# Where the fifth form of a Strassen-like product is summed in the first block of a gated Fourier/SwiGLU kernel, and where raw blocks of x lie

## The chip, the cores and the metric

One core of a Trainium2 chip runs the whole program. The metric is the device time of one execution in microseconds; before the change its median over three runs is 712.95 (712.55 to 713.23). One more execution was recorded by the hardware profiler: it took 713.02, and the instructions in its trace span 711.3.

TensorE (PE in the profile) multiplies, VectorE (DVE) and ScalarE (ACT) prepare operands and read results, GpSimd (POOL) and SyncE (SP) issue the DMAs here.

## The reference

```python
g = sigmoid((x * gate_w).sum(-1, keepdims=True))
a = x @ Wd_re.T ; b = x @ Wd_im.T               # transform along the hidden dimension
y = Ws_re @ a - Ws_im @ b                       # along the sequence, real part
h = silu(x @ w1) * (x @ w3) ; m = h @ w2        # SwiGLU
out = g * y + (1 - g) * m
```

x has 2048 rows of 512 columns, w1 and w3 are 512 x 1376, w2 is 1376 x 512, Ws 2048 x 2048 and Wd 512 x 512, all in float32.

## The kernel before

**Products.** Every float32 operand is split into a high part (ScalarE copies it into the matmul's reduced float32 format, L108) and a low part (VectorE subtracts, L111). A product is then three matmuls: high by high, high by low, low by high, in this order (`mm3`, L117). Each matmul has 512 moving columns. The large products are done in a Strassen-like way: of a 2 x 2 partition of the operands, seven products of sums of blocks instead of eight of blocks.

**Stages.** First the SwiGLU's w1 and w3 products with the gate run (`gate_up`, up to about 217 us of the trace). Then follow eight blocks: four F blocks (the transform along the sequence, applied to x), two H blocks (the w2 product) and two Y blocks (the transform along the hidden dimension). The change is in F block 0, which begins at 217.9 us.

**A block.** A block is the list `CHAIN` (L587): P1 with form B11, P5 with T1, P6 with T2, P3 with B22, P7 with T3, P2 with B21, P4 with T4. The moving operand comes from the DFT matrix `cc`: the raw blocks B11, B12, B22, B21, each in four pairs q = 0 to 3 (tiles 128 x 1024, 512 KB, called `B` in the profile). A step is one product with one q: 12 matmuls. So block 0 has steps 0 to 27: P1 is steps 0 to 3, P5 4 to 7, P6 8 to 11, P3 12 to 15, P7 16 to 19, P2 20 to 23, P4 24 to 27. The parts of a form's step, tile `zo`, have four buffers.

**Order.** The order of each engine is written out by hand. After step m's matmuls, `advance(m)` (L673) loads raw blocks for up to eight steps ahead if buffers are free, does the sum for step m + 4 (`sum_c`) and the split for step m + 3 (`split_c`). Other work is tied to a step of a block with `at` and comes ahead of the step's matmuls.

**Forms.** T1 = B12 + B11 and T2 = T1 + B22 are formed in B12's buffer by VectorE. T3 = B12 + B22. In blocks 1 to 7 VectorE forms it as T2 - B11 in B11's buffer (L649). In block 0 B11's buffer is given back as early as T1, and T3 is formed by a DMA: once B22 is split, GpSimd's queue issues a load of B12 from `cc` that adds into B22's buffer (L663). ScalarE splits that buffer for steps 16 to 19 when the DMA has landed.

**Raw blocks of x.** The stationary operands of block 0's last products and of later blocks are made from the eight raw blocks of x, `xs0` to `xs7` (128 x 1024, source `xn`): `load_a2(p)` at step 4 + p issues the load on SP's queue into a buffer of the common list `F4` (`wide`), and `make_a2(p)` at step 8 + p does the sum S3 on VectorE (128 x 256, L168), then ScalarE and VectorE split 512 and 256 columns into `a2_p` (called `a` in the profile). The three parts are in `forms2` (L165).

**Results.** At the end of P3 (step 15), P7 (step 19) and later products VectorE adds partial results and multiplies by the gate (`zu`, L862 and L772; tags u2, u3, c21, s1, p5 of the pool `ut`).

Of the kernel before, what the change touches and what calls it, by code (L numbers as in the profile page):

```python
# [7 lines left out]
F32 = mybir.dt.float32  # L8
# [4 lines left out]
P = 128  # L13
# [8 lines left out]
NG = NST // 2  # L22
# [10 lines left out]
def fnet_swiglu_gate_kernel(  # L33
# [20 lines left out]
    nc = tc.nc  # L54

    def pool(name, bufs, side, space=None):
        kw = {} if space is None else {"space": space}
        cm = tc.tile_pool(name=name, bufs=bufs, side=side, reuse_waits="tile", **kw)
        return cm, cm.__enter__()
# [30 lines left out]
    def take(places, shape, dtype, name):  # L90
        p, tag = at = places.pop(0)
        t = p.tile(shape, dtype, tag=tag, name=name)
        HELD[id(t)] = t, places, at
        return t

    def wide(name):
        return take(F4, [P, 1024], F32, name)

    def parts(name):
        return take(ZO, [P, 2, 4, 256], F32R, name)  # L100

    def free(*tiles):
        for t in tiles:
            _, places, at = HELD.pop(id(t))
            places.append(at)
# [7 lines left out]
    def split(hi, lo, src):  # L113
        high(hi, src)
        low(hi, lo, src)
# [18 lines left out]
    def flat(ap):  # L134
        return ap.rearrange("p a n -> p (a n)")
# [22 lines left out]
    def sums1_here(r):  # L158
# [3 lines left out]
        for d, v, w in ((a21, a22, a11), (a12, a12, a21)):  # L162
            nc.vector.scalar_tensor_tensor(d, v, -1.0, w, op0=ALU.mult, op1=ALU.subtract)

    def forms2(r, t2):  # L165

        r = r.rearrange("p (a n) -> p a n", a=4)
        nc.vector.tensor_sub(r[:, 0], r[:, 1], r[:, 0])  # L168
        split(flat(t2[:, 0, 0:2]), flat(t2[:, 1, 0:2]), flat(r[:, 2:4]))
        split(t2[:, 0, 2], t2[:, 1, 2], r[:, 0])  # L170

# [363 lines left out]
    A1, A2, XR = [], [], {}  # L535
# [17 lines left out]
    for n in range(NI):  # L553
        if n in W2_AT:
            p = W2_AT.index(n)
# [4 lines left out]
        if n in A1_AT:  # L560
            p = A1_AT.index(n)
# [13 lines left out]
    do(at_end, NI - 2, load_a, NG - 1)  # L575
    do(early, NI - 1, lambda: sums1_here(XR[NG - 1]))
    do(mid, NI - 1, lambda: split_c(0))
    do(at_end, NI - 1, lambda: split_c(1))


# [12 lines left out]
    NQ = [{"F": NG // 2, "H": NP2 // 2, "Y": KD // 2}[k] for k in KIND]  # L593
# [5 lines left out]
    NEED.append((("B11", 0, 0), ("B21", 1, 0), ("B12", 2, 1), ("B22", 3, 1)))  # L599
    PLACE = {"T1": "B12", "T2": "B12", "T4": "B12", "T3": "B11"}  # L600

    DONE = {"T4": "B21"}, {"T4": "B12", "B22": "B22", "T3": "B11"}
    DONE0 = {"T1": "B11", "T4": "B21"}, {"T4": "B12", "T3": "B22"}
    LEAD = 3
# [4 lines left out]
    RAW, ZT = {}, {}  # L609
# [6 lines left out]
    def block(blk, k, q):  # L616
        if KIND[blk] == "F":
            return cc[blk, ("B11", "B12", "B22", "B21").index(k), q]
        if KIND[blk] == "H":
            return hsp[blk - NTB, ("B11", "B12", "B21", "B22").index(k), q]  # L620
        return z_rows(2 * (blk - NTB - 2) + (k in ("B12", "B22")), 2 * (k in ("B21", "B22")) + q)

    def cols(blk, q, form):

        return 512 if KIND[blk] == "H" and q == NQ[blk] - 1 and form in ("B21", "B22", "T4") else 1024

    def done(m, j):
        blk, q, k, form = STEPS[m]
        b = (DONE if blk else DONE0)[j].get(form)
        if b:  # L630
            free(RAW.pop((blk, b, q)))

    def place(blk, form):
        return "B22" if form == "T3" and not blk else PLACE.get(form, form)

    def sum_c(m):


        if not 0 <= m < len(STEPS):
            return  # L640
        blk, q, k, form = STEPS[m]
        b = {"T1": "B11", "T2": "B22", "T4": "B21"}.get(form)
        if b:
            n = cols(blk, q, b)
            t = RAW[blk, PLACE[form], q][:, :n]
            nc.vector.tensor_add(t, t, RAW[blk, b, q][:, :n])  # L646
        elif form == "T3" and blk:
            t = RAW[blk, "B11", q]
            nc.vector.tensor_sub(t, RAW[blk, "B12", q], t)  # L649
        done(m, 0)  # L650

    def split_c(m):

        if not 0 <= m < len(STEPS):
            return
        blk, q, k, form = STEPS[m]
        src = RAW[blk, place(blk, form), q]
        ZT[m] = parts(f"zo{m}")
        t = ZT[m].rearrange("p h a n -> p h (a n)")
        n = cols(blk, q, form)  # L660
        split(t[:, 0, :n], t[:, 1, :n], src[:, :n])
        if form == "B22" and not blk:
            nc.gpsimd.dma_start(src, block(blk, "B12", q), accum_op=ALU.add)  # L663
        done(m, 1)

# [7 lines left out]
    def advance(m):  # L673
        load_c(m + LEAD + AHEAD)
        sum_c(m + LEAD + 1)
        split_c(m + LEAD)
# [12 lines left out]
    ut_cm, ut = pool("ut", 1, "right")  # L689
    F4[:0] = [(f4_b, f"f4_{k}") for k in range(5 + LOOK, 13)]  # L690
    ZO[:0] = [(zo_b, f"zo_{k}") for k in range(2, 4)]
    def load_a2(p):

        XR[p] = wide(f"xs{p}")
        nc.sync.dma_start(XR[p], xn[p])

    def make_a2(p):
        A2.append(a2.tile([P, 2, 3, 256], F32R, tag=f"a2_{p}", name=f"a2_{p}"))
        forms2(XR[p], A2[p])
        free(XR.pop(p))  # L700

    GATES = {}

# [181 lines left out]
    def at(blk, n, f, *a):  # L885
        todo.setdefault(START[blk] + n, []).append((f, a))

    at(1, 1, load_score, 1)
    for p in range(NG):
        at(0, 4 + p, load_a2, p)  # L890
        at(0, 8 + p, make_a2, p)
    at(0, 4, gates, 0)
    at(1, 3, gates, 1)
    late = [(w2, w2sp, p) for p in range(len(W2_AT), NP2)] + [(dd, dsp, p) for p in range(KD)]
    for i, (src, sp, p) in enumerate(late):
        blk, b = 1 + i // 2, i % 2
# [85 lines left out]
```

## Time and profile before

| | us |
|---|---|
| median of three runs | 712.95 |
| the profiled execution | 713.02 |
| its span in the trace | 711.3 |
| TensorE busy in the span | 705.0 |
| VectorE busy | 600.9 |
| ScalarE busy | 369.4 |
| GpSimd busy | 67.5 |

The granted TensorE clock is full all through. Times in the views are microseconds from the span's start. A row of the timeline gives start, length, engine, source line, operation, tiles and a count; in brackets stands how long the engine was idle before, and what ended that. An operation's stated length can overlap the next one's start, so what it costs in a row of operations is the distance of the starts.

### The profile page before, as it was taken

How to read it: one execution, taken by the hardware profiler on the slowest of the kernel's cores; microseconds unless marked ns; L12 is line 12 of the kernel's file. 1: busy time of each engine (PE TensorE's matmuls, PEld its weight loads, DVE VectorE, ACT ScalarE, POOL GpSimd, SP SyncE). 2: the span in 40 equal slices, each digit the busy share in tenths (PEclk: the TensorE clock that was granted, in tenths of full speed). 3: DMA queues.
4: the chain of work that ended last, by engine and by line, in shares of the span. 5: the costliest groups of instructions: out<-in, count | busy, mean ns of one | idle time of the engine just before them, and what ended most of it. 6: DMA issues, size and time to landing. Idle time of an engine off the chain costs nothing.

```text
span 711.3 us, 8601 instructions
## 1 busy us (share of the span) xinstructions
PE 705.0 (99%) x3089; PEld 578.4 (81%) x3089; DVE 600.9 (84%) x729; ACT 369.4 (52%) x477; POOL 67.5 (9%) x122
## 2 busy tenths in 40 slices
PE   9999999999999999999999999999999999999997
PEld 5888888888888877888888888888888888888886
DVE  6979988787679889887999599969997896898985
ACT  6665555655445665354554553544445345445451
POOL 0011111221110010000110001100110000000000
PEclk9999999999999999999999999999999999999999
DMA  7585556599997498812496228915999971773932
GB/s 280 194 296 212 213 190 253 183 314 360 417 412 270 179 242 328 302 60 88 152 360 273 89 83 336 364 37 201 362 417 416 369 266 62 295 277 140 323 119 89
DMA packets 45980, 174.64 MB, mean 246 GB/s; under 512 B 5361, under 2 KB 5489, under 8 KB 42097
## 3 DMA queue, kind: packets, MB, share of 16 engines
q1 hardware_dynamic: 32464, 118.50, 45.5%
q0 software_dynamic: 13184, 55.07, 20.4%
q8 instruction: 24, 0.39, 0.2%
q10 hardware_dynamic: 288, 0.52, 0.2%
q14 instruction: 20, 0.16, 0.1%
HBM read 116.92 MB, written 57.16 MB: 245 GB/s over the span
## 4 chain that ended last, share of the span: by engine, by line
PE 91%; issue 5%; DMA 3%; DVE 0%; POOL 0%; ACT 0%; SPq 0%; POOLq 0%; ACTq 0%
PE P L119 61%; PE X L119 16%; PE Z L119 8%; PE Y L119 4%; PE C L119 2%; DMA B<-cc 1%; DMA p5g<-gs 1%; DMA xs_B<-xt 1%; DVE zo L111 0%; ACT zo L108 0%; POOL B L663 0%; DVE xo L111 0%; DVE zc L783 0%; ACT xo L108 0%; POOL gsp L723 0%
## 5 line engine op out<-in xcount | busy, mean ns | idle before, releaser
L119 PE MATMUL P<-zo,a 128*128 128x512 f32 x1344 | 306.6, 390 | 0.8 <-DVE zo L111 0.8
L119 PEld LDWEIGHTS P<-zo,a 128*128 128x128 f32 x1344 | 251.7, 188 | 55.5 <-DVE zo L111 3.3
L108 ACT ACTIVATE zo<-B 128x1024 fp32r<-128x1024 f32 (+1 forms) x182 | 188.9, 1044 | 180.9 <-PE P L119 93.3
L111 DVE TENSOR_TENSOR zo<-B,zo 128x1024 fp32r<-128x1024 f32 (+1 forms) x182 | 218.0, 1206 | 52.4 <-ACT zo L108 51.8
L119 PE MATMUL P<-zo,H 128*128 128x512 f32 x468 | 106.2, 389 | 0.0
L119 PEld LDWEIGHTS P<-zo,H 128*128 128x128 f32 x468 | 87.8, 188 | 18.2
L646 DVE TENSOR_TENSOR B<-B,B 128x1024 f32<-128x1024 f32 (+1 forms) x78 | 93.2, 1195 | 0.1
L119 PE MATMUL X<-xo,wb 128*128 128x512 f32 x378 | 92.6, 389 | 0.0
L119 PEld LDWEIGHTS X<-xo,wb 128*128 128x128 f32 x378 | 71.0, 188 | 14.7
L119 PE MATMUL P<-zo,Y 128*128 128x512 f32 x336 | 76.3, 389 | 0.0
L119 PEld LDWEIGHTS P<-zo,Y 128*128 128x128 f32 x336 | 63.1, 188 | 13.1
L319 POOL DMA_DIRECT2D hsp<-h x42 | 23.0, 548 | 126.7 <-DVE h L370 75.8
L119 PE MATMUL X<-xo,wa 128*128 128x512 f32 x126 | 32.3, 389 | 0.0
L119 PE MATMUL Z<-xo,wa 128*128 128x512 f32 x126 | 32.3, 390 | 0.0
L119 PE MATMUL Y<-xo,wa 128*128 128x512 f32 x126 | 32.2, 389 | 0.0
L119 PE MATMUL Z<-xo,wb 128*128 128x512 f32 x126 | 32.1, 389 | 0.0
L364 DVE TENSOR_TENSOR u<-u,X 128x512 f32<-128x512 f32 x21 | 14.4, 688 | 17.9 <-PE X L119 15.6
L858 ACT ACTIVATE zu<-P 128x512 f32<-128x512 f32 x32 | 19.0, 597 | 19.2 <-PE P L119 19.2
L119 PEld LDWEIGHTS Z<-xo,wa 128*128 128x128 f32 x126 | 23.6, 188 | 5.3 <-DVE xo L111 0.4
L119 PEld LDWEIGHTS Y<-xo,wa 128*128 128x128 f32 x126 | 23.7, 188 | 4.9
L119 PEld LDWEIGHTS X<-xo,wa 128*128 128x128 f32 x126 | 23.7, 188 | 4.9
L119 PEld LDWEIGHTS Z<-xo,wb 128*128 128x128 f32 x126 | 23.7, 188 | 4.9
(134 smaller groups left out, 558.3 us busy)
## 6 DMA issues: line engine op xcount, KB each, us to landing
B<-cc SPq DMA_DIRECT2D x64, 512.0 KB, 6.8
hsp<-h POOLq DMA_DIRECT2D x42, 256.0 KB, 3.6
B<-hsp SPq DMA_DIRECT2D x20, 512.0 KB, 10.4
wbsp<-wb POOLq DMA_DIRECT2D x8, 1024.0 KB, 4.4
wb<-wbsp SPq DMA_DIRECT2D x8, 1024.0 KB, 7.7
B<-zsp SPq DMA_DIRECT2D x16, 512.0 KB, 8.3
H<-w2sp SPq DMA_DIRECT2D x6, 1024.0 KB, 10.1
ws<-w SPq DMA_DIRECT2D x11, 512.0 KB, 6.9
```

Of the source, the lines that this page charges most:

```text
L108: nc.scalar.activation(hi, src, AF.Copy)
L111: nc.vector.tensor_sub(lo, src, hi.bitcast(F32))
L119: nc.tensor.matmul(ps, u, v, start=first and n == 0, stop=last and n == 2, skip_group_check=chain)
L319: nc.gpsimd.dma_start(hsp[g, b + k, j // 2, :, j % 2 * 512 : (j % 2 + 1) * 512], h)
L364: nc.vector.tensor_add(u4, u4, x)
L646: nc.vector.tensor_add(t, t, RAW[blk, b, q][:, :n])
L858: nc.scalar.activation(U[name][:, r], ps[r], AF.Copy)
```

## The change

1. `by_dma(blk, q)` is true only for block 0 with q = 0 and 1. For q = 2 and 3 T3 is now T2 - B11 by VectorE, as in other blocks; two of the four accumulating DMAs go. For these pairs B11's buffer is held until T3's split, and B22's is given back after its own split.
2. S3 of xs(p) moves from the head of `forms2` at step 8 + p to a function of its own, `sum2`, at step 7 + p.
3. xs0 and xs4 are loaded into the tile with tag u3 of the results' pool, xs1 and xs5 into c21; xs2, xs3, xs6 and xs7 stay in `F4`. The load of xs4 must wait until xs0 has been split, that of xs5 for xs1.

```diff
+    def sum2(r):
+        nc.vector.tensor_sub(r[:, :256], r[:, 256:512], r[:, :256])
     def forms2(r, t2):
         r = r.rearrange("p (a n) -> p a n", a=4)
-        nc.vector.tensor_sub(r[:, 0], r[:, 1], r[:, 0])
         split(flat(t2[:, 0, 0:2]), flat(t2[:, 1, 0:2]), flat(r[:, 2:4]))
         split(t2[:, 0, 2], t2[:, 1, 2], r[:, 0])
...
+    def by_dma(blk, q):
+        return not blk and q < NQ[0] // 2
     def done(m, j):
         blk, q, k, form = STEPS[m]
-        b = (DONE if blk else DONE0)[j].get(form)
+        b = (DONE0 if by_dma(blk, q) else DONE)[j].get(form)
         if b:
             free(RAW.pop((blk, b, q)))
-    def place(blk, form):
-        return "B22" if form == "T3" and not blk else PLACE.get(form, form)
+    def place(blk, q, form):
+        return "B22" if form == "T3" and by_dma(blk, q) else PLACE.get(form, form)
...
-        elif form == "T3" and blk:
+        elif form == "T3" and not by_dma(blk, q):
             t = RAW[blk, "B11", q]
             nc.vector.tensor_sub(t, RAW[blk, "B12", q], t)
...
-        src = RAW[blk, place(blk, form), q]
+        src = RAW[blk, place(blk, q, form), q]
...
-        if form == "B22" and not blk:
+        if form == "B22" and by_dma(blk, q):
             nc.gpsimd.dma_start(src, block(blk, "B12", q), accum_op=ALU.add)
...
     def load_a2(p):
-        XR[p] = wide(f"xs{p}")
+        XR[p] = (flat(ut.tile([P, 2, 512], F32, tag=("u3", "c21")[p % 4], name=f"xs{p}"))
+                 if p % 4 < 2 else wide(f"xs{p}"))
         nc.sync.dma_start(XR[p], xn[p])
     def make_a2(p):
         A2.append(a2.tile([P, 2, 3, 256], F32R, tag=f"a2_{p}", name=f"a2_{p}"))
-        forms2(XR[p], A2[p])
-        free(XR.pop(p))
+        r = XR.pop(p)
+        forms2(r, A2[p])
+        if p % 4 > 1:
+            free(r)
...
     for p in range(NG):
         at(0, 4 + p, load_a2, p)
+        at(0, 7 + p, lambda p=p: sum2(XR[p]))
+    for p in range(NG):
         at(0, 8 + p, make_a2, p)
```

## The prediction

> **What bounds the kernel now.** I read the page's first lines, then the waits of the engines in block 0, then the timeline of TensorE.
>
> ```profile
> span 711.3 us, 8601 instructions
> PE 705.0 (99%) x3089; PEld 578.4 (81%) x3089; DVE 600.9 (84%) x729; ACT 369.4 (52%) x477; POOL 67.5 (9%) x122
> ```
>
> TensorE sets the end: it is idle for 711.3 - 705.0 = 6.3 us, and a gain can come only from stalls inside its row of matmuls. An undisturbed row, out of the chain that ended last, gives the pace; three rows of TensorE's timeline (one window up to 271, one from there) show where it is broken.
>
> ```profile
> 203.09 2.72 PE X L119 x12
> ...
> 261.69 9.34 PE L119 MATMUL P<-zo,a 128*128 128x512 f32 x37
> ...
> 270.57 0.47 PE L119 MATMUL P<-zo,a 128*128 128x512 f32 x1
> 271.80 8.45 PE L119 MATMUL P<-zo,a 128*128 128x512 f32 x36 [0.76 <-DVE zo L111]
> ```
>
> Twelve matmuls, one step, take 2.72 us: 0.2267 us each. From 261.69 the 37 matmuls of the first row include the one at 270.57: 36 distances in 8.88 us, where 36 x 0.2267 = 8.16 would do, so 0.72 us was lost in small pieces; the next start, at 271.80, comes 1.23 after, 1.00 too late. Together **1.72 us** between steps 16 and 19. The matmul that starts at 271.80 is the second of step 19, the first that reads the step's low part. Without the stalls it would start at 270.08, and the second matmul of step m at 270.08 - 2.72 x (19 - m): step 16 at 261.92, step 17 at 264.64, step 18 at 267.36.
>
> Who is late? The waits between 241 and 272 us (waiting tile and line, releaser; total, times, longest), and one turn of VectorE's and ScalarE's timeline in the steps in which a raw block of x is prepared:
>
> ```profile
> ACT a L108 <- DVE xs L168: 7.8, 7, 1.1
> DVE zo L111 <- ACT zo L108: 4.2, 9, 0.5
> ACT zo L108 <- DMA B<-cc: 2.8, 1, 2.8
> ```
>
> ```profile
> 241.54 1.22 DVE L646 TENSOR_TENSOR B<-B,B 128x1024 f32<-128x1024 f32 x1
> 242.68 1.22 DVE L111 TENSOR_TENSOR zo<-B,zo 128x1024 fp32r<-128x1024 f32 x1
> 243.81 0.42 DVE L168 TENSOR_TENSOR xs<-xs 128x256 f32<-128x256 f32 x1
> 244.15 1.02 DVE L111 TENSOR_TENSOR a<-xs,a 128x512 fp32r<-128x512 f32 x2
> 245.67 1.23 DVE L111 TENSOR_TENSOR zo<-B,zo 128x1024 fp32r<-128x1024 f32 x1 [0.50 <-ACT zo L108]
> 246.81 0.42 DVE L168 TENSOR_TENSOR xs<-xs 128x256 f32<-128x256 f32 x1
> ...
> 248.67 1.23 DVE L111 TENSOR_TENSOR zo<-B,zo 128x1024 fp32r<-128x1024 f32 x1 [0.50 <-ACT zo L108]
> ...
> 266.66 1.22 DVE L111 TENSOR_TENSOR zo<-B,zo 128x1024 fp32r<-128x1024 f32 x1 [0.51 <-ACT zo L108]
> 267.80 1.28 DVE L862 TENSOR_TENSOR zu<-zu,P 128x512 f32<-128x512 f32 x2
> 269.00 1.29 DVE L772 TENSOR_TENSOR zu<-zu,gate 128x512 f32<-128x512 f32 x2
> 270.51 4.63 DVE L111 TENSOR_TENSOR zo<-B,zo 128x1024 fp32r<-128x1024 f32 x4 [0.23 <-ACT zo L108]
> ```
>
> ```profile
> 245.54 0.62 ACT L108 ACTIVATE a<-xs 128x512 fp32r<-128x512 f32 x1
> 247.27 0.42 ACT L108 ACTIVATE a<-xs 128x256 fp32r<-128x256 f32 x1 [1.11 <-DVE xs L168]
> 247.59 1.05 ACT L108 ACTIVATE zo<-B 128x1024 fp32r<-128x1024 f32 x1
> ```
>
> The two engines wait in a ring: S3 (246.81) lets ScalarE do the 256-column high part (247.27), behind which stands the step's own high part (247.59), for which VectorE's low part waits (248.67), behind which stands the next S3. A turn takes 248.67 - 245.67 = **3.00 us**, against TensorE's 2.72. Over eight turns VectorE loses 2.2 us, the lead is used up, and the low parts of steps 16 to 18 come late (the 0.72). Step 19's comes latest of all; the chain that ended last goes through it (start, length, what):
>
> ```profile
> 259.31 10.00 DMA B<-cc
> ...
> 269.42 1.07 ACT zo L108
> ...
> 270.51 1.24 DVE zo L111
> ```
>
> Its high part waited for the fourth accumulating DMA, landed at 269.31 (2.8 us on ScalarE), and its low part stands behind four `zu` operations. Of those two the DMA explains only the last 0.23 us; without it VectorE would have started at 270.28, still too late.
>
> **The change, part by part.** The built program's order per engine leaves TensorE and ScalarE as they were; VectorE and the queues change.
>
> *S3 a step ahead.* Number and length stay, eight of 0.42 us. ScalarE finds the sum done, so the ring is open: no wait of 1.1 and none of 0.50. VectorE then costs its own work per step, in distances of starts: S3 0.34 (243.81 to 244.15), the two low parts of x 0.60 (two `zu` take 1.20, 267.80 to 269.00) and 0.34, the step's low part 1.14 (245.67 to 246.81): 2.42 us, now *under* 2.72. ScalarE's share of a turn is 0.62 + 0.42 + 1.05 = 2.09 us: it keeps ahead.
>
> *T3 by VectorE for q = 2 and 3.* Two more operations, in the place before steps 17 and 18's low parts. Their like in later blocks:
>
> ```profile
> L649 DVE TENSOR_TENSOR B<-B,B 128x1024 f32<-128x1024 f32 x22 | 26.8, 1219 | 0.0
> ```
>
> 1.22 us, 1.14 from start to start, so 2.28 us more VectorE work. What hides it is the lead won by the first edit. To check, I add up VectorE's new order from 241.54, a start the change does not move, to the end of step 19's low part: one T2 sum, ten low parts of steps 10 to 19 and two T3 are 13 x 1.14 = 14.82; eight S3 and eight 256-column low parts 16 x 0.34 = 5.44; eight 512-column low parts and four `zu` 12 x 0.60 = 7.20; 0.09 for the last one's full length. Sum 27.55: done at **269.09**, needed at 270.08, 0.99 us to spare. On the way: step 16's low part is done at 258.8 (needed 261.92), step 17's at 262.3 (264.64), step 18's at 265.5 (267.36). So no stall, if VectorE never waits more than 0.99 us in all. Without the lead (ring still closed) the two operations would cost their 2.28 in full.
>
> *Two accumulating DMAs fewer.* This removes ScalarE's wait for the fourth. The first two stay, and come earlier.
>
> ```profile
> 250.33 0.89 POOL L663 DMA_DIRECT2D B<-cc  x1 [13.91 <-DVE xs L168]
> 253.32 0.87 POOL L663 DMA_DIRECT2D B<-cc  x1 [2.10 <-DVE xs L168]
> ...
> DMA to landing us min/median/max: 6.0/6.0/6.0
> ...
> DMA to landing us min/median/max: 8.5/8.5/8.5
> ```
>
> They land 6.0 and 8.5 us after issue (the line's own view, a window for each): at 256.3 and 261.9, the fourth at 269.3, on average 3.7 after the one before it, so they run one behind the other. POOL issues 0.43 us after the low part of step 12 ends (248.67 + 1.23 = 249.90 against 250.33). That low part moves to 247.9, so the first is issued at 249.5, 0.8 earlier, and the second at 251.9. As the second queues behind the first, I move its landing by the 0.8 only: 261.1. Bounds: 257.9 (251.9 + 6.0, no queue) and 261.9 (no gain). From landing to the end of step 19's low part: 1.2 for the high part (269.31 to 270.51 in the chain), then 4 x 1.14 (step 17, T3, steps 18 and 19), 0.94 of x, 2.40 of `zu`, 0.09: 9.2 us. So 270.3 with 261.1, **0.2 us past** 270.08; nothing with 257.9; 1.0 us with 261.9. I take 0.2: landings 3.7 to 5.6 us apart, for issues 3.0 apart, speak for a queue.
>
> *Buffers.* The raw blocks' loads on SP:
>
> ```profile
> 222.05 9.45 SPq L695 DMA_DIRECT2D xs<-xn  x5
> 238.22 0.33 SPq L799 DMA_DIRECT2D gate<-gsp  x1
> 245.20 6.32 SPq L695 DMA_DIRECT2D xs<-xn  x3
> 254.19 30.78 SPq L671 DMA_DIRECT2D B<-cc  x14
> ...
> DMA to landing us min/median/max: 3.3/6.3/9.8
> ...
> DMA to landing us min/median/max: 3.3/3.4/3.4
> ```
>
> xs0 and xs1 go out sooner. xs4, so far among the first five (done by 231.5), now waits for xs0's split: 245.5 (241.54, two S3, one T2 sum, step 10's low part, 0.94 of low parts). Behind it stand the gate's load (from 238.2 to 245.9; first read at 269.00), xs5 (248.0), xs6, xs7, then B21 and block 1. xs4's sum comes at 251.4, 5.9 us after the issue, xs5's at 253.8, 5.8 after. The first landing line is that of all eight loads, the second that of the two issued between 244 and 249 alone, 3.3 to 3.4; so I cost this at nothing, hidden under VectorE's own order. B11 held longer for two pairs takes two buffers, the x blocks in u3 and c21 give two back; B21's first load moves from 254.2 to about 252.8.
>
> A rule of the Trainium skill speaks against the change: "VectorE: DVE Perf Modes", section "The DRAIN you can't avoid", says that the next operation does not start until the pipe has emptied. By it each would cost its full length, and the time would be that of rival (e). The rows here say otherwise, 1.22 us operations start 1.14 apart, and the same page grants an earlier start to operations that are not held; the sum goes by the rows.
>
> **Sum.** 1.72 saved, 0.2 of it back: 713.02 - 1.5 = 711.5 for a profiled execution; the median of three lies 0.07 lower: **711.4**. Without the 0.2 it is 711.2.
>
> **The rivals.**
>
> (a) *The wait moves to the second accumulating DMA.* It lands no earlier than before, 261.9, or later. For: the DMA engines carry xs5, xs6, xs7 and B21 beside it, as before or closer. Against: two accumulations fewer behind it. Step 19 is then 1.0 us late: gain 0.7, 712.2; with another 0.5 us of delay 712.7.
>
> (b) *The change doesn't do what it says: nothing is won.* The 0.50 waits go, but T3's 2.28 and other small waits (step 19 behind `zu`) use the lead up: 2.7 us of waits in all bring step 19 to 271.8. 712.9. Against: no releaser for them in the rows.
>
> (c) *Slower: xs4 comes late.* It decides from a landing at 252.4 (251.4 plus the 0.99 to spare), 6.9 us after issue. At the longest landing in the row, 9.8, it is 255.3: VectorE waits 3.9, step 19's low part ends at 273.0, 2.9 late: 1.2 more than before, 714.1. For: the median landing of these loads is 6.3. Against: the long ones were queued behind up to four others, at 245.5 only the gate follows.
>
> (d) *Slower: the ring stays closed*, ScalarE's wait of 1.11 having another cause than S3. Then the 2.28 come on top of the 3.00 turns: 715.2. Against: the sum ends at 247.23 and ScalarE starts at 247.27.
>
> (e) *Every operation at full length:* 13 x 1.22 + 16 x 0.42 + 12 x 0.69 = 30.9 us, 272.4, stall 2.3: 713.5. The distances of 1.14 are against it. This is the result that the rule of the Trainium skill's page would give.
>
> **How the numbers follow.** Forecast 0.66, (a) 0.18, (b) 0.05, (c) 0.05, (d) 0.04, (e) 0.02. The forecast's own range is 711.0 to 711.7, with the runs' spread of 0.35 on either side 710.7 to 712.0. To leave out no more than 2 in 10 I take in (a) with its bound: **710.7 to 712.8**. The bound of 0.2%, about what a measurement of this kernel can tell from no change, is 1.43 us, and the forecast gains 1.55: so of its 0.66 0.55 is faster and 0.11 same. Of (a) 0.04 faster (early landing), 0.14 same; (b) same; (c) half and half; (d) slower; (e) same. Faster 0.60, same 0.33, slower 0.07.
>
> **What would show it.** Right: no wait of `a` for `xs` on ScalarE, `zo` 2.42 apart in steps 11 to 16, TensorE in one row from 221 us on with less than 0.3 us lost up to step 19; two L663 instead of four, landing before 261.2; VectorE's L168 successor runs without a wait for a DMA. Wrong: a bracket on ScalarE's `zo` for the DMA longer than VectorE's spare; `xs4` landing after 252.4; turns of 3.0 still. A new stall of TensorE in steps 20 to 27 would be something I do not see in these rows.

## The result, and the profile after

| | before | after |
|---|---|---|
| median, us (14 runs each) | 713.25 | 712.31 |
| lowest to highest | 712.55 to 715.46 | 711.62 to 713.53 |
| ratio, with 95% interval | | 0.9985 [0.9978, 0.9992] |
| the profiled execution | 713.02 | 712.41 |
| its span in the trace | 711.3 | 710.6 |

The change makes the kernel 0.15% faster, 0.94 us by the medians. The same kernel was timed once more beside the last experiments: 712.88 (11 runs) against 713.33, 0.9993 [0.9984, 1.0002]. The predicted range, 710.7 to 712.8, holds the first median, and the second lies 0.08 above it; the forecast, 711.4, is 0.9 below the first, and 712.31 is almost the 712.2 of rival (a). The interval of the first comparison leaves out 1, that of the second does not. In the traces of both the gain is about half of what was to be had, as the rows below show.

The page's first lines of the changed kernel (busy time, share of the span, instructions):

```profile
span 710.6 us, 8590 instructions
PE 704.8 (99%) x3089; PEld 578.7 (81%) x3089; DVE 602.4 (85%) x731; ACT 369.0 (52%) x477; POOL 65.7 (9%) x120
```

VectorE has its two operations more, GpSimd two DMAs less. TensorE's rows in block 0 (start, length, what, count; in brackets the idle time and its end) show where the time goes:

```profile
218.12 52.55 PE L119 MATMUL P<-zo,a 128*128 128x512 f32 x229
271.19 29.09 PE L119 MATMUL P<-zo,a 128*128 128x512 f32 x127 [0.52 <-DVE zo L111]
```

The break is still at the second matmul of step 19, where it was before (217.89 and 271.80 there). Block 0 began 0.23 us later in this execution, so the fair measure is the distance from the block's first matmul to that one: **53.91 us before, 53.07 after**. The prediction's undisturbed time is 270.08 - 217.89 = 52.19. So 1.72 us was lost before, and 0.88 is lost now: 0.84 gained, where 1.5 was forecast. From the break on the two executions are alike: the last row of the chain that ended last starts there and is 435.69 us long (435.70 before).

```profile
271.19 435.69 PE P L119 x1919
```

All experiments below are read by this distance, since the time up to block 0 differs between executions.

What is VectorE late for? Its timeline in steps 11, 12 and 16 to 19, from rows that the prediction summed up:

```profile
245.65 1.23 DVE L111 TENSOR_TENSOR zo<-B,zo 128x1024 fp32r<-128x1024 f32 x1
246.79 0.42 DVE L167 TENSOR_TENSOR xs<-xs 128x256 f32<-128x256 f32 x1
247.12 1.03 DVE L111 TENSOR_TENSOR a<-xs,a 128x512 fp32r<-128x512 f32 x2
248.06 1.23 DVE L111 TENSOR_TENSOR zo<-B,zo 128x1024 fp32r<-128x1024 f32 x1
...
257.69 1.23 DVE L111 TENSOR_TENSOR zo<-B,zo 128x1024 fp32r<-128x1024 f32 x1
...
260.10 1.23 DVE L656 TENSOR_TENSOR B<-B,B 128x1024 f32<-128x1024 f32 x1
263.16 1.22 DVE L111 TENSOR_TENSOR zo<-B,zo 128x1024 fp32r<-128x1024 f32 x1 [1.84 <-ACT zo L108]
...
269.91 4.63 DVE L111 TENSOR_TENSOR zo<-B,zo 128x1024 fp32r<-128x1024 f32 x4
```

The ring is open: the step's low part comes every 2.41 us (245.65, 248.06, ... 257.69: five turns in 12.04), no bracket stands in these rows, and after step 16's low part at 257.69 VectorE is ahead of TensorE. Then it stands still for 1.84 us ahead of step 17's low part (263.16), and all that follows is late by that much. ScalarE, for which it waits, waited itself; the queue that it waited for, GpSimd's, had issued in good time:

```profile
256.54 1.06 ACT L108 ACTIVATE zo<-B 128x1024 fp32r<-128x1024 f32 x1 [1.65 <-DMA B<-cc]
...
262.07 1.06 ACT L108 ACTIVATE zo<-B 128x1024 fp32r<-128x1024 f32 x1 [3.64 <-DMA B<-cc]
```

```profile
249.72 0.88 POOL L671 DMA_DIRECT2D B<-cc  x1 [13.07 <-DMA gate<-gsp]
252.12 0.85 POOL L671 DMA_DIRECT2D B<-cc  x1 [1.52 <-DVE xs L167]
```

```profile
DMA to landing us min/median/max: 9.8/9.8/9.8
```

The last line is from the issue line's own view, for the second of the two alone (from issue to landing). It went out at 252.12 and landed at 261.96, 43.85 us after the block's first matmul; before, the second landed 43.98 after it, though it was issued 1.4 us later by that clock (253.32 - 217.89 = 35.43 against 34.00). The wait moved to the second accumulating DMA.

### The profile page after: what moved, and what is told of

It is laid out like the page before. It is cut to its first block, busy times and chain, and to the rows that moved or that the text cites. A ratio compares the mean times of both kernels' runs of the same rounds, so it can differ in the third digit from the quotient of the medians.

```text
span 710.6 us, 8590 instructions
## 1 busy us (share of the span) xinstructions
PE 704.8 (99%) x3089; PEld 578.7 (81%) x3089; DVE 602.4 (85%) x731; ACT 369.0 (52%) x477; POOL 65.7 (9%) x120
## 3 DMA queue, kind: packets, MB, share of 16 engines
q1 hardware_dynamic: 32464, 118.50, 45.2%
q0 software_dynamic: 12896, 54.02, 19.7%
## 4 chain that ended last, share of the span: by engine, by line
PE 90%; DVE 4%; DMA 3%; ACT 1%; issue 1%; SPq 0%; POOL 0%; ACTq 0%; DVEq 0%; POOLq 0%
PE P L119 61%; PE X L119 16%; PE Z L119 8%; PE Y L119 4%; DVE zo L111 2%; DMA B<-cc 1%; PE C L119 1%; DVE B L653 1%; DMA xs_B<-xt 1%; ACT zo L108 1%; DMA gate<-gsp 0%; DVE a L111 0%; ACT L730 0%; DVE xo L111 0%; DVE B L656 0%
## 5 line engine op out<-in xcount | busy, mean ns | idle before, releaser
L870 ACT ACTIVATE zu<-P 128x512 f32<-128x512 f32 x32 | 19.0, 597 | 20.3 <-PE P L119 20.3
L656 DVE TENSOR_TENSOR B<-B,B 128x1024 f32<-128x1024 f32 x24 | 29.3, 1219 | 0.0
```

What stands on the lines that cost most here:

```text
L870: nc.scalar.activation(U[name][:, r], ps[r], AF.Copy)
```

## The experiments

Two accounts were tried. By the first, *the landing*, VectorE's order fits as the prediction summed it, and only an accumulating DMA that lands late breaks it; what delays that landing is the other traffic, the loads of x and of B21 from SP's queue. By the second, *VectorE's total*, its order is too long with T3's two operations, and the DMA is a bystander. In the recorded expectations Theory V is the second account. Theory Q is the first, as are the two theories of what sets a landing: contention (the loads beside it) and queue (each accumulation takes its time of its own queue, whatever runs beside it). "Accumulations land" stands for the time after block 0's first matmul, in us. e1 to e11 are the names that the expectations use.

| kernel | first matmul to step 19's second | accumulations land | median (runs) | ratio to before |
|---|---|---|---|---|
| before | 53.91 | 38.45, 43.98, 47.58, 51.43 | 713.25 to 713.33 | |
| after | 53.07 | 38.32, 43.85 | 712.31 (14) | 0.9985 [0.9978, 0.9992] |
| after, again | 53.08 | 40.08, 43.86 | 712.88 (11) | 0.9993 [0.9984, 1.0002] |
| S3 ahead, x in results' tiles, four DMAs (e1) | 56.40 | 42.54, 46.29, 50.14, 53.92 | 715.34 (6) | 1.0029 [1.0018, 1.004] |
| T3 and tiles, S3 not ahead (e2) | 54.67 | 38.17, 43.91 | 713.78 (10) | 1.0007 [0.9998, 1.0016] |
| S3 ahead alone (e8) | 53.36 | 38.27, 43.25, 47.05, 50.88 | 712.73 (10) | 0.9991 [0.9982, 1.0] |
| one DMA (e3) | 52.66 | 37.73 | 711.59 (10) | 0.9977 [0.9968, 0.9987] |
| B21 late (e5) | 52.19 | 38.88, 42.91 | 711.39 (10) | 0.9975 [0.9966, 0.9984] |
| B21 late, again (e5) | 52.74 | 39.98, 42.68 | 712.41 (11) | 0.9984 [0.9975, 0.9993] |
| four DMAs, B21 late (e11) | 52.17 | 40.37, 43.26, 45.70, 48.87 | 711.56 (10) | 0.9974 [0.9965, 0.9983] |
| `zu` of P3 late (e6) | 52.96 | 40.42, 44.41 | 712.32 (11) | 0.9982 [0.9973, 0.9991] |
| B21 and `zu` late (e10) | 52.43 | 39.92, 43.89 | 711.64 (8) | 0.9973 [0.9963, 0.9984] |
| one DMA, `zu` late (e7) | 52.19 | 37.31 | 711.40 (10) | 0.9974 [0.9965, 0.9984] |

### The parts alone

**S3 ahead and x in results' tiles, all four accumulating DMAs kept.** Against the changed kernel:

```diff
-        return not blk and q < NQ[0] // 2
+        return not blk
```

> S3 a step ahead and the new places of the x blocks, but all four T3 of block 0 by accumulating DMA. Measure: the time from block 0's first matmul to the second of step 19, which is 53.91 us before, 53.07 after, and 52.14 without stalls from step 2 on. Theory Q (the accumulating DMAs run one behind the other and set the end): the fourth lands at 269 to 270 as before, step 19's low part follows 2.4 later, so 53.6 to 54.0 and a time within 0.3 us of before. Rival R (the closed ring alone cost the time, and opening it is the whole gain): about 53.1 or less, as after, and 0.9 us faster than before.

Measured: 56.40, worse than before by 2.5 us, 715.34. Both accounts missed this. TensorE's rows, then SP's and GpSimd's, then the DMA line's view for its four issues:

```profile
217.67 44.25 PE L119 MATMUL P<-zo,a 128*128 128x512 f32 x193
262.69 3.02 PE L119 MATMUL P<-zo,a 128*128 128x512 f32 x12 [0.76 <-DVE zo L111]
266.44 3.08 PE L119 MATMUL P<-zo,a 128*128 128x512 f32 x12 [0.73 <-DVE zo L111]
270.29 3.03 PE L119 MATMUL P<-zo,a 128*128 128x512 f32 x12 [0.77 <-DVE zo L111]
274.07 26.15 PE L119 MATMUL P<-zo,a 128*128 128x512 f32 x114 [0.75 <-DVE zo L111]
```

```profile
247.72 1.28 SPq L705 DMA_DIRECT2D xs<-xn  x3
249.04 25.33 SPq L679 DMA_DIRECT2D B<-cc  x9
```

```profile
249.27 0.89 POOL L671 DMA_DIRECT2D B<-cc  x1 [13.07 <-DMA gate<-gsp]
```

```profile
DMA to landing us min/median/max: 10.9/11.7/13.7
```

Each of the steps 16 to 19 now waits for its own accumulation, 12 matmuls and a stall, 3.8 us apart. The buffers that this kernel frees (B11's, and those of four x blocks) let SP's queue go on: all three x loads are out by 249.0 and B21's first load goes out at 249.04, ahead of the first accumulation (249.27). In the changed kernel the loads of x take until 250.91 and B21 begins only at 252.99 (rows in the prediction's points below). With these loads beside them the accumulations land 10.9 to 13.7 us after their issue. No VectorE total explains that: VectorE has no T3 to form here.

**T3 by VectorE and x in results' tiles, S3 not ahead.**

```diff
     def make_a2(p):
         A2.append(a2.tile([P, 2, 3, 256], F32R, tag=f"a2_{p}", name=f"a2_{p}"))
         r = XR.pop(p)
+        sum2(r)
         forms2(r, A2[p])
...
-        at(0, 7 + p, lambda p=p: sum2(XR[p]))
```

> T3 of pairs 2 and 3 by VectorE and the new places of the x blocks, but S3 back in the step of its splits. If the ring of ScalarE and VectorE is what S3 ahead opens: turns of 3.0 us again, each T3 fills 0.50 of a wait and costs 0.64 more, its like in front of step 18 too, so step 19's low part ends about 1 us later than before: 54.7 to 55.0 from first matmul to step 19, and 0.8 to 1.1 us slower than before. Rival: the ring costs nothing once the DMAs are gone: 53.1, as after.

Measured: 54.67, 0.76 worse than before, just under the 54.7 to 55.0 expected; 713.78, 0.45 above before where 0.8 to 1.1 was expected, 1.0007 [0.9998, 1.0016]. VectorE's rows:

```profile
257.86 1.23 DVE L111 TENSOR_TENSOR zo<-B,zo 128x1024 fp32r<-128x1024 f32 x1 [0.48 <-ACT zo L108]
...
260.86 1.23 DVE L111 TENSOR_TENSOR zo<-B,zo 128x1024 fp32r<-128x1024 f32 x1 [0.50 <-ACT zo L108]
...
263.27 1.22 DVE L656 TENSOR_TENSOR B<-B,B 128x1024 f32<-128x1024 f32 x1
264.41 1.22 DVE L111 TENSOR_TENSOR zo<-B,zo 128x1024 fp32r<-128x1024 f32 x1
...
267.95 1.22 DVE L111 TENSOR_TENSOR zo<-B,zo 128x1024 fp32r<-128x1024 f32 x1
```

The ring turns in 3.00 us as before (257.86 to 260.86); with T3 in the turn it is 3.55 (260.86 to 264.41, and 3.54 to 267.95), and there VectorE works without a break. Here its total sets the end: T3 pays only behind the lead that S3 wins.

**S3 ahead alone**, a `sum2` at step 7 + p, in the kernel before:

```diff
+    def sum2(r):
+        nc.vector.tensor_sub(r[:, :256], r[:, 256:512], r[:, :256])
...
-        nc.vector.tensor_sub(r[:, 0], r[:, 1], r[:, 0])
...
+        at(0, 7 + p, lambda p=p: sum2(XR[p]))
+    for p in range(NG):
```

> The kernel before with S3 a step ahead and nothing else: x blocks in the common buffers, four accumulating DMAs. In run e1, with x blocks in the results' tiles, 56.40 passed from first matmul to step 19. If e1 was slow because the freed buffers let B21's loads go out beside the accumulations (from 249.0 instead of 254.2), here those loads keep near their times (252.7 or later), the accumulations land no later than before, and 53.0 to 54.0 pass. If instead S3 ahead with four accumulations is slow in itself, 56 and more again.

Measured: 53.36, 0.55 gained; 712.73, 0.9991 [0.9982, 1.0]. TensorE breaks once, at step 19, whose accumulation is the fourth and lands at 50.88 (51.43 before). So two thirds of the whole change's gain in the trace is this one moved operation; the tiles and T3 bring the other 0.3. (The interval of its ratio reaches 1.0: the medians alone do not settle a gain of this size.)

From the first experiment this kernel differs in one thing, the place of the x blocks, and it is 3.0 us faster up to step 19 (53.36 against 56.40). B21's first load goes out 34.88 us after the block's first matmul here and at 31.37 there. So it is the x blocks' new places, and nothing that VectorE does, that made the first experiment slow.

### What delays the landing

**One accumulating DMA fewer**, T3 of q = 1 to 3 by VectorE. For lack of a buffer xs6 and xs7 come a step later.

```diff
-        return not blk and q < NQ[0] // 2
+        return not blk and q < 1
...
-        at(0, 4 + p, load_a2, p)
+        at(0, 4 + p + (p > 5), load_a2, p)
```

> Only pair 0's T3 by accumulating DMA, three by VectorE; xs6 and xs7 are loaded a step later because a buffer is held longer. Theory Q: no wait for a second accumulation; VectorE's own order ends step 19's low part 1.14 later than the sum without waits, 0.15 after TensorE wants it: 52.3 to 52.4 from first matmul to step 19 (after: 53.07), 0.7 to 0.8 us faster than after, about 711.5. Theory V (VectorE's total work sets the stall, the DMA wait only fills it): 1.14 more work gives 54.0 to 54.2, 0.9 to 1.1 us slower than after.

Measured: 52.66, and 711.59. VectorE has a third operation of 1.14 us and the kernel is *faster* by 0.4 us in the trace, 0.7 in the medians: its total is refuted as the cause. Of the 0.47 that is still lost, 0.15 is VectorE's own work (1.14 less the 0.99 us to spare of the prediction's sum). The kernel is 0.3 short of what the landing's account asked, and the waits (waiting tile and line, releaser; total, times, longest) show where:

```profile
ACT zo L108 <- DMA B<-cc: 1.1, 1, 1.1
...
DVE xs L167 <- DMA xs<-xn: 0.3, 1, 0.3
```

VectorE waits 0.3 us for xs6, which this edit loads later. That is a new wait of the experiment, not one of the change.

**B21 late.** Block 0's four loads of B21 are issued by ScalarE, three steps later for q = 0, two for q = 1, one for q = 2. They stand behind step 17's high part in its order, so none goes out before the second accumulation has landed. VectorE's order is that of the changed kernel.

```diff
-    LOADS = sorted((START[blk] + n * nq - e * (blk > 0 or n != 1) + q, blk, k, q)
+    LOADS = sorted((START[blk] + n * nq - e * (blk > 0 or n != 1) + q
+                    + (3 - q) * (blk == 0 and k == "B21"), blk, k, q)
...
-            nc.sync.dma_start(r[:, :n], block(blk, k, q)[:, :n])
+            e = nc.scalar if blk == 0 and k == "B21" else nc.sync
+            e.dma_start(r[:, :n], block(blk, k, q)[:, :n])
```

> The changed kernel, but block 0's four B21 loads are issued by ScalarE behind step 17's high part, so that no load of B21 runs beside the two accumulations (in the changed kernel four are issued between 253 and 259). Contention theory: without these loads the second accumulation lands 2 to 4 us earlier, at 258 to 260, step 17's high part doesn't hold VectorE, and 52.3 to 52.6 us pass from block 0's first matmul to step 19. Queue theory: an accumulation takes some 4 to 5 us of its queue whatever runs beside it, the landing stays between 261 and 262, and 52.9 to 53.1 pass.

Measured: 52.19, no stall at all, and 711.39. The second accumulation lands at 42.91, 0.94 earlier. That is less than the 2 to 4 us expected, and enough for the stall. TensorE's timeline has one row:

```profile
218.59 81.66 PE L119 MATMUL P<-zo,a 128*128 128x512 f32 x358
```

Run once more beside the changed kernel it did less well:

> Run e5 once more (B21's loads behind step 17's high part). In e5 the second accumulation landed 42.91 us after block 0's first matmul, but in e10, with the same loads, 43.89. Contention theory: 42.8 to 43.5, no stall over 0.1 us at step 19, 0.6 to 0.9 us faster than after_again. If the landing only varies from execution to execution: 43.5 or later, 52.9 or more from first matmul to step 19, and the time within 0.3 us of after_again's.

Measured: 52.74, 712.41, still 0.47 us below the changed kernel's 712.88 in the same comparison (0.6 to 0.9 expected). The second accumulation lands early again (42.68), but the *first* came at 39.98 where it had come at 38.88 us, and VectorE waited for that one:

```profile
258.89 1.23 DVE L111 TENSOR_TENSOR zo<-B,zo 128x1024 fp32r<-128x1024 f32 x1 [1.51 <-ACT zo L108]
```

1.51 of wait less the 0.99 that VectorE had to spare (its cover) is 0.52; TensorE lost 0.55. The first accumulation is not brought forward by B21's delay: 38.88, 39.98 and 39.92 us with two DMAs and B21 late, 38.32 and 40.08 in the changed kernel.

**The change itself, again**, unchanged:

> The changed kernel once more, beside the two below on one chip. The second accumulation landed 43.85 us after block 0's first matmul in the first profile and 44.41 in run e6, whose order is the same up to there. If its landing sets the stall: 43.7 to 44.5, and from first matmul to step 19 53.0 to 53.7; about 0.9985 of before.

Measured: 53.08, the same 0.9 us lost, and 712.88. The second accumulation landed at 43.86 (43.85 the first time), the first at 40.08 (38.32 the first time). So VectorE now waits ahead of step 16's low part too. Its rows, then ScalarE's two:

```profile
259.06 1.23 DVE L111 TENSOR_TENSOR zo<-B,zo 128x1024 fp32r<-128x1024 f32 x1 [1.61 <-ACT zo L108]
...
261.48 1.22 DVE L656 TENSOR_TENSOR B<-B,B 128x1024 f32<-128x1024 f32 x1
262.84 1.23 DVE L111 TENSOR_TENSOR zo<-B,zo 128x1024 fp32r<-128x1024 f32 x1
```

```profile
257.97 1.06 ACT L108 ACTIVATE zo<-B 128x1024 fp32r<-128x1024 f32 x1 [3.41 <-DMA B<-cc]
...
261.75 1.06 ACT L108 ACTIVATE zo<-B 128x1024 fp32r<-128x1024 f32 x1 [1.89 <-DMA B<-cc]
```

Step 17's low part starts 1.36 us after T3, where 1.14 would do: ScalarE's high part, which waited for the second accumulation, ends only at 262.81. Counted from the block's first matmul it starts at 45.06, in the first execution at 45.04. The second landing sets the end both times, and the wait of 1.61 at step 16, worth 0.6 us by itself, is hidden behind it.

Either of the two accumulations can use up the cover of 0.99 us: the second did in the changed kernel, the first in B21's repetition. What makes the first land 1.8 us later in one execution than in another of the same kernel stays open: no run separates it.

**Four DMAs with B21 late**, the first experiment's edit and B21's together, tells most about the cause:

> Run e1 (S3 ahead, x blocks in the results' tiles, four accumulating DMAs, 56.40 from first matmul to step 19) with B21's loads behind step 17's high part. Contention theory: the accumulations no longer run beside B21's loads, the first lands 3 us or more earlier than e1's 260.2, and 53.0 to 54.0 pass: most of e1's 2.5 us loss against before goes. Queue theory: four accumulations take 4 to 5 us each whatever runs beside them, and 55.5 or more stay.

Measured: 52.17 up to step 19 (0.29 is lost at step 23), faster than the 53.0 to 54.0 expected, and 711.56 against 715.34 with B21 on time. The first accumulation lands 2.2 us earlier than in the first experiment, where 3 or more were expected. Rows of GpSimd and the line's view of its four issues:

```profile
251.73 0.89 POOL L672 DMA_DIRECT2D B<-cc  x1 [13.07 <-DMA gate<-gsp]
...
260.81 0.84 POOL L672 DMA_DIRECT2D B<-cc  x1 [3.40 <-issue]
```

```profile
DMA to landing us min/median/max: 8.2/9.0/9.3
```

Same four accumulations, same S3, same buffers for x: with B21's loads out of the way the fourth lands at 48.87 instead of 53.92, and the four come 2.4 to 3.2 us apart instead of 3.8. 3.78 us of median go with it. With B21 on time three plain loads of `cc` land between the first and the fourth accumulation (at 44.86, 48.72 and 52.49); with B21 late none does. The loads beside the accumulations set how far apart these land.

Part of the fourth's gain is an earlier issue. In both kernels GpSimd issues it 0.31 us after the first has landed (42.85 after 42.54, and 40.68 after 40.37), behind a wait for which the profile shows no releaser (`<-issue`); from issue to landing it then takes 11.1 and 8.2 us. (This profiled execution came to block 0 at 220.12, 2.0 us later than the changed kernel's first one, and took 713.68 against its median of 711.56; the distances within block 0 are read from it, the time is not.)

### Room elsewhere

**P3's `zu` late**: VectorE's add and gate product at the end of P3 run after the next step's `advance`, behind step 19's low part.

```diff
+    LATER = {}
...
+        if m in LATER:
+            LATER.pop(m)()
...
-        if k == "P1":
+        if k == "P3" and not blk:
+            def add(b=blk, p=ps):
+                for r in range(2):
+                    nc.vector.tensor_add(U["u2"][:, r], U["u2"][:, r], p[r])
+                spill(b, 2, U["u2"])
+            LATER[m + 1] = add
+        elif k == "P1":
```

> The changed kernel, with the four zu operations of P3's end behind step 19's split instead of in front of it. If step 19's low part is late only because the second accumulation's late landing leaves VectorE no time for the zu operations (2.40 us) ahead of it, it now ends 2.4 us earlier, at about 268.7, before TensorE wants it at 270.3: 52.2 to 52.4 us from block 0's first matmul to step 19 (0.17 may stay at step 18), about 0.8 us faster than the changed kernel. Rival: a wait elsewhere takes its place (step 20's part, or the zsp store), and 52.9 to 53.1 stay.

Measured: 52.96, 712.32. The 2.40 us of `zu` are gone from ahead of step 19 and its stall with them, yet nothing is won: in this execution the accumulations landed at 40.42 and 44.41, and TensorE loses its time at steps 17 and 18, before the point that the edit helps. Too late a landing can't be made good by room behind it.

**B21 and `zu` late together:**

> The changed kernel with both B21's loads behind step 17's high part (run e5: 52.19) and the zu operations behind step 19's split. Either alone should leave no stall to remove, so both together give 52.14 to 52.25 and no time below e5's beyond the spread, about 711.4. If e5's gain was something else than the early landing, the two add up: 0.5 us or more below e5.

Measured: 52.43, 711.64. No better than B21 alone, as it should be where both remove the same stall. The second accumulation landed at 43.89 here, no earlier than in the changed kernel: B21's delay brought that landing forward by 0.9 and 1.2 us in two executions and not at all in a third, a mean of 0.7. That the plain loads lengthen accumulations is shown with four of them; what moving B21 earns with two differs from execution to execution.

**One DMA with `zu` late**, both edits as above:

> One accumulating DMA (run e3: 52.66 from first matmul to step 19, of which 0.16 is VectorE's own work and 0.3 a wait for a late raw x block) and the zu operations behind step 19's split. VectorE has 2.4 us more for step 19's low part, and nothing waits for a second accumulation: 52.14 to 52.25, and 711.2 to 711.5, no faster than e5, since no stall is left there either. If VectorE's total work were the limit, step 20 to 23 would stall instead, 0.3 us or more.

Measured: 52.19, no stall, the 0.3 us wait for xs6 now covered; 711.40, 0.9974 [0.9965, 0.9984], against 0.9993 [0.9984, 1.0002] for the changed kernel in the same comparison. It is faster than both kernels, and depends on one landing instead of two:

```profile
218.05 82.28 PE L119 MATMUL P<-zo,a 128*128 128x512 f32 x361
```

360 distances of 0.2267 and one length of 0.39 are 82.0; all but 0.3 us of the row is matmuls back to back. A version with no accumulating DMA wasn't tried.

## Why the prediction was near and its forecast was not

*The stall and its place* held. 1.72 us was lost before; with all stalls of this place gone (B21 late in its first execution; one DMA with `zu` late) the distance is 52.19, the prediction's own 270.08 - 217.89, and the medians are 711.39 and 711.40, 1.9 us under before. So its sum without the returned part, 711.2, was the right size for what there was to gain.

*The ring* held: turns of 2.41 us (2.42 forecast). ScalarE's wait of `a` for `xs` didn't vanish but fell from 7.8 us in seven to 1.0 in three (waits from 241 to 275), with nothing behind it:

```profile
ACT zo L108 <- DMA B<-cc: 5.3, 2, 3.6
...
DVE zo L111 <- ACT zo L108: 1.8, 1, 1.8
...
ACT a L108 <- DVE xs L167: 1.0, 3, 0.5
```

*VectorE's order* held: from 241.78 to the end of step 19's low part (269.91 + 1.23) are 29.36 us; less the wait of 1.84, 27.52, where 27.55 was added up. So no other waits add up, as rival (b) had it. By full lengths it would be 30.9, so rival (e) is out. The result that the rule in "The DRAIN you can't avoid" of the Trainium skill's "VectorE: DVE Perf Modes" would give if it held for each operation, 713.5, wasn't borne out: these operations start 1.13 to 1.14 us apart at a stated length of 1.22. Rival (d) said what T3 costs without the lead, 2.2 us slower; with S3 not ahead it was 0.76. The turn grew by 0.55 for each T3, not by 1.14, since VectorE's waits of 0.5 in the ring hid the rest, and the wait of 0.23 for the fourth DMA was gone.

*The buffers* held. SP's rows:

```profile
220.11 25.98 SPq L705 DMA_DIRECT2D xs<-xn  x5
246.19 0.38 SPq L811 DMA_DIRECT2D gate<-gsp  x1
248.18 2.73 SPq L705 DMA_DIRECT2D xs<-xn  x3
252.99 31.38 SPq L679 DMA_DIRECT2D B<-cc  x14
```

xs4, last of the five, went out at 245.8 (245.5 forecast, 0.23 of that the later start), landed 3.3 us later, and no wait of `xs` for a DMA stands among the waits: rival (c) is out. B21 began at 252.99 (252.8 forecast).

*The accumulations' issue* held: 249.72 and 252.12, less 0.23 the forecast 249.5 and 251.9.

*From landing to the end* held: 9.2 us forecast from the second landing to the end of step 19's low part, 9.17 measured (261.97 to 271.14).

*The second landing failed.* The step reads "I move its landing by the 0.8 only: 261.1", 43.21 us after the block's first matmul. Measured: 43.85 and 43.86, nearly as late as the bound of 261.9 (44.01), which the prediction wrote down and didn't take. In the first execution the second follows the first by 5.53 us, as before. It is the first that failed to come earlier: issued 0.84 us earlier by the block's clock (31.60 against 32.44), it landed 0.13 earlier (38.32 against 38.45). The term that was mis-sized is **what the landing gives back: 0.2 us forecast, 0.88 measured**. That is rival (a) by its own number: step 19 about 1.0 late, 712.2. The reason was in its text too, under "for": the DMA engines carry the loads beside it, "as before or closer". The price of that was in no sum. An earlier issue was taken to be an earlier landing, for DMAs whose landings, 3.6 to 5.5 us apart in four issues 3.0 apart, did not follow their issue; and the change that issues them earlier also frees the buffers that let SP's loads go out earlier. With S3 ahead alone, where no x block has moved, the second is issued at 34.00 like here and landed at 43.25, almost the 43.21 of the prediction. That is one execution, but it points at the loads that the new places let go earlier: B21's second pair goes out at 36.01 in the changed kernel, at 37.28 there. That such loads decide is shown with four DMAs: 53.92 against 48.87 for the same fourth DMA. Which of them, x's or B21's, cost the second landing of the changed kernel how much was not separated.

*The first landing* is not safe either, though the prediction has no cost for it: 38.32 in one execution and 40.08 in the next. With B21 late it was the whole stall of one execution (0.55); in the changed kernel it stayed hidden behind the second.

The gain of 0.94 in the medians against 0.84 in the trace, and 0.45 when repeated, is within what runs differ; the forecast's bound of 0.2% is not reached in either.

## What to carry to other kernels

An earlier issue of a DMA need not be an earlier landing when other queues have work ready: before a term is costed by "issue plus the old duration", ask which loads the same change releases at that moment, and take the end of the bounds at which nothing is gained unless a row shows otherwise. Freed buffers are traffic: the same edit, keeping four accumulating DMAs, lost 2 us with B21 on time and won 1.8 with B21 late. When an engine has a small cover (0.99 us here) against a landing that varies by more than that between executions, take the DMA off its path (one instead of two, the work on the engine that has the room) rather than move it.

## What the runs showed of the hardware that was not expected

An accumulating DMA costs the DMA engines more than a plain one of the same size. Queue lines of the profile's page (packets, MB, share of 16 engines' span), of the kernel before and then of the one after:

```profile
q0 software_dynamic: 13184, 55.07, 20.4%
```

```profile
q0 software_dynamic: 12896, 54.02, 19.7%
q1 hardware_dynamic: 32464, 118.50, 45.2%
```

Two accumulations of 0.52 MB less are 0.7% of 711 us, 5.0 us, so some 2.5 us of all sixteen engines each (the rounding of the shares leaves 0.35 either way). The other profiles agree: q0 has 20.3% to 20.4% with four accumulations, 19.7% to 19.8% with two and 19.3% with one. SP's plain loads take 45.2% of 710.6, 321 us, for 118.50 MB: 1.4 us for 0.52 MB. Both are estimates from shares; they go with the spacings, 2.4 to 3.2 us with little beside them and 3.8 beside plain loads.

The landing of one and the same DMA in the same order of instructions varies between executions far more than the whole kernel's time: 38.32 and 40.08 us for the first accumulation of the changed kernel, whose two profiled executions differ by 0.34 us in all (712.41 and 712.07). And the start of block 0 falls between 217.7 and 218.6 us in the traces, with 220.12 in one, which is why single executions were compared from block 0's first matmul on.
